# Sigmoid attention in 128-row chunks, with the last 64 rows of four heads as one float32 step in quarters of TensorE

## The chip, the cores and the metric

The kernel runs on one core of one Trainium2 chip. The metric is the device time of one execution in microseconds (us). Before the change three runs took 1105.21 to 1106.7 us, median 1105.92.

## The reference

Eight batches of twelve heads go through sigmoid attention, and the result through a two-layer perceptron with a gate. All inputs and outputs are float32 (the perceptron's weights reach the kernel as 64-bit floats and are decoded in it).

```
q, k, v: (8, 12, 448, 64)
scores = q @ k.T / sqrt(64) - log(448)
attn   = 1 / (1 + exp(-scores))
x      = (attn @ v), heads side by side: (3584, 768)
h      = x @ w_in                        # (768, 2048)
out    = (h / (1 + exp(-1.702 h))) @ w_out   # (2048, 768)
```

## The kernel before

Attention works on 48 pairs of heads, in the order of batches, six pairs in each. A pair's q and k lie side by side in one tile of 128 rows (two heads of 64 dimensions) by 896 columns, first the 448 of q, then the 448 of k. `split_pair` turns it into two float32r tiles, the rounded values (line 347) and the rest (line 358), both on VectorE; the first pair of all is used unrounded, in plain float32. A product of two split operands is then three float32r products: rest by rounded, rounded by rest, rounded by rounded.

k is cut into four chunks of 112 rows. For each chunk `scores` (line 541) multiplies the chunk, as weights of 64 rows by 112 columns, with q, for both heads: one head in the upper half of TensorE's rows, one in the lower, into two PSUM banks. That is six matmuls in a chunk. ScalarE applies the sigmoid to both heads at once (line 552), and `values` (line 564) multiplies the result with v in plain float32, one head in the left half of TensorE's columns and one in the right, with 112 rows. A profile shows each float32 matmul as two. The four chunks accumulate in one bank, whose two halves of rows are then the output of the two heads; ScalarE or VectorE copies it out into `x32` tiles (lines 598 and 600, `to_x`), which are stored to memory (`xd`).

A unit of work on TensorE is the four score chunks of one pair and behind them the four value chunks of the pair before. Scores and outputs take turns at four places of two PSUM banks each (`two_banks`).

Between the pairs the kernel decodes the perceptron's weights (lines 408 to 442, 32 pieces, each loaded by a transfer of 768 KB into one of three buffers `raw64`), forms sums of some of them (line 683) and stores the results. A load of weights is tied to the progress of the pairs by `PACE`. The order of all instructions on each engine and of the transfers on the SP queue is fixed when the kernel is built: `Plan.run` plays the tasks through with a cost for each and emits them in that order. So an instruction that waits holds back all that stand behind it on its engine. Tiles that come from a ring (`BUFS` has the sizes) wait for the last user of the tile that had the place.

Behind attention comes the perceptron, first for one block of 512 tokens (lines 716), then for pairs of blocks with fewer products (lines 952 and 1093). Its first products need six tiles `x0_0` to `x0_5`, loaded back from memory and split as well (lines 347 to 358).

## Time and profile before

| what | value |
|---|---|
| median of three runs | 1105.92 us |
| the profiled execution, its span | 1107.12 us, 1105.3 us |
| TensorE, VectorE, ScalarE busy in the span | 99%, 69%, 46% |
| granted TensorE clock | 1.00 |
| score matmuls (line 541) | 1128 in float32r, 127.3 us |
| value matmuls (line 564) | 768 records, 154.7 us |
| sigmoids of attention (line 552) | 192, 183.0 us |
| first perceptron product on TensorE | at 285.26 us |

Busy times of TensorE are those of overlapping matmuls. The page names engines PE (TensorE), PEld (its weight loads), DVE (VectorE), ACT (ScalarE) and SPq (the queue that issues transfers). A group of instructions reads: line, engine, operation, output<-inputs, shapes, count, busy time, mean ns of one, idle time of the engine just before and what ended it.

### The profile page before, as it was taken

The page shows a single profiled execution, that of the slowest core. Times are in us where ns is not written, and L with a number is a line of the kernel's source. Part 1 is how long each engine was busy: PE and PEld are TensorE (multiplying, and loading weights), DVE is VectorE, ACT ScalarE, POOL GpSimd, SP SyncE. Part 2 cuts the span into 40 slices and gives each one's busy share as a digit, 9 for nine tenths or more (in the row PEclk, how much of TensorE's full clock was granted, in tenths as well). Part 3 has the DMA queues.
Part 4 walks back from the last instruction along what each step waited for, and adds up shares of the span by engine and source line. Part 5 has one row for each costly group of instructions (what it writes and reads, how often), then busy time and mean ns, then how long its engine had stood idle before and what let it go on. Part 6 is the DMA issues. An engine that isn't in the chain of part 4 may idle for free.

```text
span 1105.3 us, 14979 instructions
## 1 busy us (share of the span) xinstructions
PE 1098.0 (99%) x5538; PEld 826.1 (75%) x5538; DVE 764.7 (69%) x1246; ACT 507.2 (46%) x717; POOL 0.2 (0%) x4
## 2 busy tenths in 40 slices
PE   9999999999999999999999999999999999999998
PEld 5455555555788888888888888888888888888887
DVE  6899999998597227887983764448955744487652
ACT  7888998888553222224532222225332222244220
POOL 0000000000000000000000000000000000000000
PEclk9999999999999999999999999999999999999999
DMA  9999999999647878676777876557679755556665
GB/s 311 324 367 358 359 390 382 374 340 336 196 161 247 312 243 296 243 257 212 233 226 249 300 236 199 194 193 240 219 228 305 254 188 190 187 182 207 201 212 187
DMA packets 113240, 285.68 MB, mean 258 GB/s; under 512 B 10384, under 2 KB 51472, under 8 KB 113168
## 3 DMA queue, kind: packets, MB, share of 16 engines
q1 hardware_dynamic: 113168, 284.73, 75.4%
q8 instruction: 44, 0.72, 0.3%
q14 instruction: 28, 0.23, 0.1%
HBM read 206.05 MB, written 78.64 MB: 258 GB/s over the span
## 4 chain that ended last, share of the span: by engine, by line
PE 95%; DMA 3%; DVE 1%; SPq 0%; issue 0%; DVEq 0%
PE os L1093 18%; PE m L952 18%; PE oa L1093 13%; PE av L564 12%; PE sc L541 10%; PE sc L952 9%; PE h L716 6%; PE o L716 6%; PE av L952 4%; DMA qkraw<-qk 2%; DMA w<-w 1%; SPq L326 0%; DVE qk L358 0%; DVE qk L347 0%; DVE expo L408 0%
## 5 line engine op out<-in xcount | busy, mean ns | idle before, releaser
L552 ACT ACTIVATE a<-sc,bias 112x896 f32<-112x896 f32 x192 | 183.0, 1005 | 33.7 <-PE av L564 19.9
L1093 PE MATMUL os<-gs,wds 128*128 128x512 f32 x864 | 196.3, 389 | 0.0
L1093 PEld LDWEIGHTS os<-gs,wds 128*128 128x128 f32 x864 | 162.2, 188 | 33.7
L564 PE MATMUL av<-a,vraw 112*64 112x448 f32 x768 | 154.7, 545 | 0.0
L1093 PE MATMUL oa<-ga,wda 128*128 128x512 f32 x648 | 147.4, 389 | 0.0
L1093 PEld LDWEIGHTS oa<-ga,wda 128*128 128x128 f32 x648 | 121.6, 188 | 25.3
L541 PEld LDWEIGHTS sc<-qk 64*112 64x112 f32 x1128 | 95.5, 171 | 48.9 <-ACT a L552 34.2
L541 PE MATMUL sc<-qk 64*112 64x448 f32 x1128 | 127.3, 370 | 2.4 <-DVE x L600 1.3
L564 PEld LDWEIGHTS av<-a,vraw 112*64 112x64 f32 x768 | 50.8, 136 | 82.7 <-issue 82.0
L952 PE MATMUL m<-x_s,w 128*128 128x512 f32 x468 | 109.3, 389 | 0.0
L952 PE MATMUL sc<-x,w 128*128 128x512 f32 x432 | 105.7, 389 | 0.0
L952 PEld LDWEIGHTS m<-x_s,w 128*128 128x128 f32 x468 | 87.8, 188 | 18.2
L952 PEld LDWEIGHTS sc<-x,w 128*128 128x128 f32 x432 | 81.1, 188 | 16.8
L914 ACT ACTIVATE g<-h 128x512 f32<-128x512 f32 x72 | 44.8, 633 | 90.6 <-DVE h L815 89.7
L352 ACT CAST gs<-gs 128x512 fp32r<-128x512 f32 x75 | 46.7, 623 | 84.3 <-PE os L1093 74.5
L716 PE MATMUL h<-x,wsplit 128*128 128x512 f32 x288 | 65.6, 389 | 0.0
L716 PE MATMUL o<-gs,wsplit 128*128 128x512 f32 x288 | 65.4, 389 | 0.0
L716 PEld LDWEIGHTS h<-x,wsplit 128*128 128x128 f32 x288 | 54.0, 188 | 11.9 <-issue 0.7
L716 PEld LDWEIGHTS o<-gs,wsplit 128*128 128x128 f32 x288 | 54.1, 188 | 11.2
L358 DVE TENSOR_TENSOR gs<-gs,gs 128x512 fp32r<-128x512 f32 x96 | 60.8, 685 | 0.4
L919 DVE TENSOR_TENSOR gs<-sc,g 128x512 f32<-128x512 f32 x24 | 16.6, 691 | 60.8 <-ACT g L914 60.8
L815 DVE TENSOR_TENSOR h<-h,m 128x512 f32<-128x512 f32 x36 | 24.7, 686 | 40.0 <-PE m L952 40.0
(93 smaller groups left out, 1237.2 us busy)
## 6 DMA issues: line engine op xcount, KB each, us to landing
w<-w SPq DMA_DIRECT2D x56, 768.0 KB, 6.7
wds<-t SPq DMA_DIRECT2D x72, 384.0 KB, 4.0
t<-t SPq DMA_DIRECT2D x32, 768.0 KB, 5.0
w<-t SPq DMA_DIRECT2D x32, 768.0 KB, 5.0
qkraw<-qk SPq DMA_DIRECT2D x47, 448.0 KB, 8.6
wda<-w SPq DMA_DIRECT2D x48, 384.0 KB, 3.9
f<-w SPq DMA_DIRECT2D x32, 384.0 KB, 5.9
w<-wsplit SPq DMA_DIRECT2D x16, 768.0 KB, 6.2
```

Source lines behind the costliest of these rows:

```text
L352: (costs[0], lambda: nc.scalar.copy(hi(), src())),
L358: lambda: nc.vector.tensor_tensor(lo(), src(), hi().bitcast(F32), op=ALU.subtract),
L541: nc.tensor.matmul(ps.tile[:C, j, :S], lhsT=src[kk][rows, S + c * C : S + (c + 1) * C], rhs=src[qq][rows, :S], start=n == 0, stop=n == len ...
L552: nc.scalar.activation(a.tile[:C, c % 2], ps.tile[:C, :, :S], AF.Sigmoid, bias=bias[:C], scale=scale)
L564: nc.tensor.matmul(ps.tile[cols, 0, :S], lhsT=vr.tile[:C, j, c], rhs=a.tile[:C, c % 2, j], start=c == 0, stop=c == NC - 1,)
L716: nc.tensor.matmul(ps, lhsT=ws[a], rhs=x[:, c], start=first and i == 0, stop=last and i == 2)
L815: nc.vector.tensor_tensor(out(), a(), b(), op=op)
L914: nc.scalar.activation(g.tile, h(), AF.Sigmoid, scale=1.702)
L919: nc.vector.tensor_tensor(gb.tile[:, block - one], h(), g.tile, op=ALU.mult)
L952: nc.tensor.matmul(ps, lhsT=ws[c], rhs=x[:, d], start=not more and i == 0 and j == 0, stop=i == NK // 2 - 1 and j == 2, skip_group_check=more,
L1093: nc.tensor.matmul(to, lhsT=w[c], rhs=x.tile[:, d], start=not more and i == 0 and j == 0, stop=i == len(rows) - 1 and j == 2, skip_group_c ...
```

## The change

Heads go by fours, as two pairs. k is cut into three chunks of 128 rows, and the 64 rows left over of each of the four heads form one further step (`scores_left`): four products with weights of 64 rows by 64 columns, each in one quarter of TensorE, in plain float32 from the raw q/k tiles, into two banks. One sigmoid serves all four. `values` works with 128 rows, and `values_left` adds the four heads' last 64 rows of v, again in quarters. The output of four heads shares one place of two banks (`bank` in `to_x`), and is copied out when `values_left` is done. v is laid out on the host so that one load brings four heads. The rounding of q and k may now go to ScalarE or VectorE. The PSUM places have new names (`q0` to `q3`), and the perceptron uses `q0` and `q1` where it used `sc`.

```diff
--- before.py
+++ after.py
@@ -34,15 +34,15 @@
 
 
 BUFS = dict(
-    qk=2, vraw=3, a=3, x32=8, x=6, g=16, line=4, wsplit=3, raw64=3, w32=2, e=4,
-    sc=2, sc3=1, sc4=1, av=1, m=2, m0=1,
+    qk=2, vraw=3, a=6, x32=8, x=6, g=16, line=4, wsplit=3, raw64=3, w32=2, e=4,
+    q0=1, q1=1, q2=1, q3=1, av=1, m=2, m0=1,
     xs=15, xa=4,
 )
 
 ATTENTION, LATE = ("qk", "vraw", "a", "raw64", "e"), ("xs", "xa")
 SHARED = ("line",)
 
-EARLY, SINGLE = ("sc3", "sc4"), ("m0", "av", "m")
+PAIRED, EARLY, SINGLE = ("q0", "q1"), ("q2", "q3"), ("m0", "av", "m")
 
 
 
...
@@ -257,8 +257,10 @@
     NW = w.shape[0]
     NF = NW * NK // (NK + NM)
 
-    NC = 4
-    C = S // NC
+    NC = S // P
+    C = S - NC * P
+
+    VC = (2 * NC + 1) * P
     NW_EL = NK * P
     scale = 1.0 / math.sqrt(D)
     neg_log_s = -math.log(S)
...
@@ -485,24 +488,29 @@
         n: [dram.tile([P, T], F32, name=f"xd{n}_{p}", tag=f"xd{n}_{p}") for p in range(NP)]
         for n in range(NB)
     }
-    spilled = {}
+    spilled, v_of = {}, {}
 
     def load_pair(b, p):
 
         tag = "x"
-        qkr, vr = buffer(tag), buffer("vraw")
-        vals, rows = v[b], C
+        qkr = buffer(tag)
+
         def first():
             if qkr.tile is None:
                 make(qkr, tag, [P, S2], F32, f"qkraw{b}_{p}")
 
 
         t_q = []
-        for cols in (slice(0, S + C), slice(S + C, S2)) if (b, p) == (0, 0) else (slice(0, S2),):
+        for cols in (slice(0, S + P), slice(S + P, S2)) if (b, p) == (0, 0) else (slice(0, S2),):
             t_q.append(dma(lambda cols=cols: qkr.tile[:, cols], lambda cols=cols: qk[b, p * P : (p + 1) * P, cols],
                            P * (cols.stop - cols.start) * 4 / 1024, [], [qkr], first))
-        t_v = dma(lambda: vr.tile[:rows], lambda: vals[:, 2 * p : 2 * p + 2], rows * 8 * D * 4 / 1024, [], [vr],
-                  lambda: make(vr, "vraw", [P, 2, NC, D], F32, f"vraw{b}_{p}"))
+
+        if p % 2 == 0:
+            vr = buffer("vraw")
+            t_v = dma(lambda: vr.tile, lambda: v[b, p // 2], P * VC * 4 / 1024, [], [vr],
+                      lambda: make(vr, "vraw", [P, VC], F32, f"vraw{b}_{p}"))
+            v_of[b, p // 2] = t_v, vr
+        t_v, vr = v_of[b, p // 2]
         return t_q, qkr, t_v, vr
 
     def split_pair(b, p, t_q, qkr):
...
@@ -510,63 +518,88 @@
             return t_q[0], qkr
         s = buffer("qk")
         t = round_and_rest(
-            (None, 0.63, 1.09), s, lambda: qkr.tile, t_q, [qkr],
+            (0.94, 0.63, 1.09), s, lambda: qkr.tile, t_q, [qkr],
             lambda: s.tile[:, 0], lambda: s.tile[:, 1],
             lambda: make(s, "qk", [P, 2, S2], F32R, f"qk{b}_{p}"),
         )
         return t, s
 
 
-    turns, last_early = itertools.count(), {}
-
-    def two_banks(b):
-        b.tag = ("sc", "sc", *EARLY)[next(turns) % 4]
-        plan.rings.setdefault(b.tag, []).append(b)
-        last_early[b.tag] = b
-
-    def scores(b, p, c, t_s, s, a):
-
-        ps = Buffer()
-        two_banks(ps)
-
-
-        plain = (b, p) == (0, 0)
-        terms = ((0, 0),) if plain else ((0, 1), (1, 0), (0, 0))
-
+    last_early = {}
+
+    def two_banks(place):
+        tag = (*PAIRED, *EARLY)[place % 4]
+        b = buffer(tag)
+        b.tag, last_early[tag] = tag, b
+        return b
+
+    def sigmoid(name, a, ps, t):
         def emit():
-            make(ps, ps.tag, [P, 2, 512], F32, f"sc{b}_{p}_{c}")
-            src = [s.tile] if plain else [s.tile[:, 0], s.tile[:, 1]]
-            for n, (kk, qq) in enumerate(terms):
+            make(a, "a", [P, 2, S], F32, name)
+            nc.scalar.activation(a.tile, ps.tile[:, :, :S], AF.Sigmoid, bias=bias, scale=scale)
+
+        return task("ACT", 1.02, emit, [t], [a, ps])
+
+    def scores(n, c, t_s, s, place):
+        ps, a = two_banks(place), buffer("a")
+
+        terms = ((0, 1), (1, 0), (0, 0)) if n else ((0, 0),)
+
+        def emit():
+            make(ps, ps.tag, [P, 2, 512], F32, f"sc{n}_{c}")
+            src = [s.tile[:, 0], s.tile[:, 1]] if n else [s.tile]
+            for i, (kk, qq) in enumerate(terms):
                 for j, rows in enumerate(halves_of_rows):
                     nc.tensor.matmul(
-                        ps.tile[:C, j, :S],
-                        lhsT=src[kk][rows, S + c * C : S + (c + 1) * C], rhs=src[qq][rows, :S],
-                        start=n == 0, stop=n == len(terms) - 1,
+                        ps.tile[:, j, :S], lhsT=src[kk][rows, S + c * P : S + (c + 1) * P], rhs=src[qq][rows, :S],
+                        start=i == 0, stop=i == len(terms) - 1,
                     )
 
-        t = task("PE", 0.9 if plain else (0.75, 0.61, 0.61, 0.61)[c], emit, t_s, [ps, s])
-
-        def sigmoid():
-            if a.tile is None:
-                make(a, "a", [P, 2, 2, S], F32, f"a{b}_{p}_{c}")
-            nc.scalar.activation(
-                a.tile[:C, c % 2], ps.tile[:C, :, :S], AF.Sigmoid, bias=bias[:C], scale=scale
-            )
-
-        return t, task("ACT", 1.02, sigmoid, [t], [a, ps])
-
-    def values(b, p, c, t_a, a, t_v, vr, ps):
+        t = task("PE", (0.7, 0.61, 0.61)[c] if n else 0.9, emit, t_s, [ps, s])
+        return t, sigmoid(f"a{n}_{c}", a, ps, t), a
+
+    def scores_left(n, sources, place):
+
+        ps, a = two_banks(place), buffer("a")
 
         def emit():
-            if c == 0:
-                make(ps, ps.tag, [P, 2, 512], F32, f"av{b}_{p}")
+            make(ps, ps.tag, [P, 2, 512], F32, f"sc{n}_{NC}")
+            for cols, (_, src) in zip(halves_of_rows, sources):
+                for j, rows in enumerate(halves_of_rows):
+                    nc.tensor.matmul(
+                        ps.tile[cols, j, :S], lhsT=src.tile[rows, S + NC * P :], rhs=src.tile[rows, :S],
+                        start=True, stop=True, skip_group_check=True,
+                    )
+
+        t = task("PE", 0.95, emit, [t for ts, _ in sources for t in ts], [ps, *(b for _, b in sources)])
+        return t, sigmoid(f"a{n}_{NC}", a, ps, t), a
+
+    def values(n, c, t_a, a, t_v, vr, ps):
+
+        def emit():
+            if ps.tile is None:
+                make(ps, ps.tag, [P, 2, 512], F32, f"av{n}")
             for j, cols in enumerate(halves_of_rows):
+                at = ((n % 2 * 2 + j) * NC + c) * D
                 nc.tensor.matmul(
-                    ps.tile[cols, 0, :S], lhsT=vr.tile[:C, j, c], rhs=a.tile[:C, c % 2, j],
-                    start=c == 0, stop=c == NC - 1,
+                    ps.tile[cols, n % 2, :S], lhsT=vr.tile[:, at : at + D], rhs=a.tile[:, j],
+                    start=c == 0, stop=False, skip_group_check=True,
                 )
 
-        return task("PE", (0.8, 0.75, 0.75, 0.85)[c], emit, [t_a, t_v], [ps, a, vr])
+        return task("PE", (0.8, 0.75, 0.75)[c], emit, [t_a, t_v], [ps, a, vr])
+
+    def values_left(t_a, a, t_v, vr, ps):
+
+        def emit():
+            for k, rows in enumerate(halves_of_rows):
+                for j, cols in enumerate(halves_of_rows):
+                    at = (4 * NC + j) * D
+                    nc.tensor.matmul(
+                        ps.tile[cols, k, :S], lhsT=vr.tile[rows, at : at + D], rhs=a.tile[rows, j],
+                        start=False, stop=True, skip_group_check=True,
+                    )
+
+        return task("PE", 0.95, emit, [t_a, t_v], [ps, a, vr])
 
     def places(b):
 
...
@@ -591,16 +624,20 @@
 
             yield block, xb, first, into, cols
 
+    copies = []
+
     def to_x(b, p, t, ps):
+        bank = (b * NP + p) % 2
         for block, xb, first, into, cols in x32_places(b, p):
             n = cols.stop - cols.start
-            wrote[block, p].append(on_either(
+            copies.append(on_either(
                 (0.2 + 0.00075 * n, lambda xb=xb, into=into, cols=cols: nc.scalar.copy(
-                    xb.tile[:, into], ps.tile[:, 0, cols])),
+                    xb.tile[:, into], ps.tile[:, bank, cols])),
                 (0.15 + 0.00105 * n, lambda xb=xb, into=into, cols=cols: nc.vector.tensor_copy(
-                    xb.tile[:, into], ps.tile[:, 0, cols])),
+                    xb.tile[:, into], ps.tile[:, bank, cols])),
                 [t], [xb, ps], first,
             ))
+            wrote[block, p].append(copies[-1])
         split_x(b, p)
 
     def split_x(b, p):
...
@@ -620,36 +657,50 @@
         ), x)
 
 
-    firsts = []
+    firsts, urgent = [], []
 
     def attention():
 
-        units, late = [], []
+
+
+
+
+
+        units, late, held = [], [], 0
         for n, (b, p) in enumerate(pairs):
             t_q, qkr, t_v, vr = load_pair(b, p)
             t_s, s = split_pair(b, p, t_q, qkr)
-            ps = Buffer()
-            scored, next_late = [], []
             firsts.append(t_s)
-            for half in range(2):
-                a = buffer("a")
-                got = [scores(b, p, c, [t_s] if n else t_q[: c + 1], s, a) for c in range(2 * half, 2 * half + 2)]
-                scored.append([g[0] for g in got])
-                next_late.append([
-                    values(b, p, 2 * half + i, g[1], a, t_v, vr, ps) for i, g in enumerate(got)
-                ])
-
-            if n:
-                two_banks(before)
-            before = ps
-
-            for t in scored[1] + [t for two in late for t in two]:
+            chunks = [scores(n, c, [t_s] if n else t_q[: c + 1], s, held + 1 + c) for c in range(NC)]
+            run = [t for t, _, _ in chunks]
+            if n % 2 == 0:
+                left, chunks0, pair0 = [(t_q, qkr)], chunks, (b, p)
+            else:
+                t_left, t_a, a = scores_left(n, [*left, (t_q, qkr)], held)
+                run.append(t_left)
+                held += 1
+                ps = two_banks(held)
+                both = [
+                    [values(m, c, got[1], got[2], t_v, vr, ps) for c, got in enumerate(cs)]
+                    for m, cs in ((n - 1, chunks0), (n, chunks))
+                ]
+                both[1].append(values_left(t_a, a, t_v, vr, ps))
+                late.append(both[0])
+                copied = len(copies)
+                for pair in (pair0, (b, p)):
+                    to_x(*pair, both[1][-1], ps)
+                urgent.append(copies[copied:])
+            if n > 2 and n % 2:
+
+                plan.early += [(t, run[0]) for t in urgent[n // 2 - 1]]
+
+            with_v = late.pop(0) if late else []
+            for t in run[2:] + with_v:
                 t.alone = False
-            units.append(scored[0] + scored[1] + [t for two in late for t in two])
-            to_x(b, p, next_late[1][1], ps)
-            late = next_late
-        two_banks(before)
-        units.append(late[0] + late[1])
+            units.append(run + with_v)
+            if n % 2:
+                late.append(both[1])
+        units.append(late.pop())
         return units
 
 
...
@@ -1183,7 +1234,12 @@
     DM, DF = moe_w_in.shape
     qk = np.concatenate([q, k], axis=2).transpose(0, 1, 3, 2)
     qk = np.ascontiguousarray(qk).reshape(B, H * D, 2 * S)
-    vl = v.reshape(B, H, 4, S // 4, D).transpose(0, 3, 1, 2, 4)
+
+
+    vh, full = v.reshape(B, H // 4, 4, S, D), S // P * P
+    chunks = vh[..., :full, :].reshape(B, H // 4, 4, full // P, P, D).transpose(0, 1, 4, 2, 3, 5)
+    ends = vh[..., full:, :].reshape(B, H // 4, 2, 2, S - full, D).transpose(0, 1, 2, 4, 3, 5)
+    vl = np.concatenate([chunks.reshape(B, H // 4, P, -1), ends.reshape(B, H // 4, P, 2 * D)], axis=3)
     vl = np.ascontiguousarray(vl)
     KB, FB = DM // P, DF // P
     wi = moe_w_in.reshape(KB, P, FB, P).transpose(2, 0, 1, 3)
```

In all, 47 roundings of q and k stood on VectorE before; now 30 do, and 17 on ScalarE. Of the copies out of PSUM 59 stood on VectorE and 25 on ScalarE; now 35 and 49. The two places that follow show the order itself.

TensorE in the middle of attention, before: `sc1_4_2` is the scores of batch 1, pair 4, chunk 2, `a` a sigmoid, `av` an output.

```order
L564 MATMUL av1_2_856<-a1_2_0_757,vraw1_2_686 64x448 x4
L564 MATMUL av1_2_856<-a1_2_2_804,vraw1_2_686 64x448 x4
L541 MATMUL sc1_4_0_878<-qk1_4_797 112x448 x6
L541 MATMUL sc1_4_1_892<-qk1_4_797 112x448 x6
L541 MATMUL sc1_4_2_900<-qk1_4_797 112x448 x6
L541 MATMUL sc1_4_3_910<-qk1_4_797 112x448 x6
L564 MATMUL av1_3_919<-a1_3_0_824,vraw1_3_753 64x448 x4
L564 MATMUL av1_3_919<-a1_3_2_867,vraw1_3_753 64x448 x4
```

The same place now: `sc13_0` is the scores of the pair numbered 13, chunk 0, and chunk 3 is the step of left-over rows; `av12` is the output of the pairs 12 and 13.

```order
L584 MATMUL av10_928<-a11_0_903,vraw1_4_650 64x448 x2
L584 MATMUL av10_928<-a11_1_916,vraw1_4_650 64x448 x2
L584 MATMUL av10_928<-a11_2_924,vraw1_4_650 64x448 x2
L597 MATMUL av10_928<-a11_3_939,vraw1_4_650 64x448 x4
L553 MATMUL sc13_0_1004<-qk2_1_926 128x448 x6
L553 MATMUL sc13_1_1017<-qk2_1_926 128x448 x6
L553 MATMUL sc13_2_1028<-qk2_1_926 128x448 x6
L569 MATMUL sc13_3_1038<-qkraw2_0_685 64x448 x2
L569 MATMUL sc13_3_1038<-qkraw2_1_687 64x448 x2
L584 MATMUL av12_1048<-a12_0_966,vraw2_0_763 64x448 x2
L584 MATMUL av12_1048<-a12_1_979,vraw2_0_763 64x448 x2
L584 MATMUL av12_1048<-a12_2_986,vraw2_0_763 64x448 x2
```

Each pair had four chunks of scores of 112 columns, then two times two chunks of values. Now it has three of 128, and in turn the left scores stand behind the chunks (`x2` for each pair's raw tile) or the left values behind the values (`x4`).

VectorE at the end of attention, before: `x32_6_2` is the copy out of a finished pair, `x0_3` the split of the perceptron's first input tiles, `w32_15` the last weights decoded.

```order
L424 TENSOR_TENSOR expo15_3205<-expo15_3205,sign15_3186 128x768
L358 TENSOR_TENSOR qk7_5_3250<-qkraw7_5_2872,qk7_5_3250 128x896
L600 COPY x32_6_2_2884<-av7_2_3247 128x448
L442 SCALAR_TENSOR_TENSOR w32_15_3200<-w32_15_3200,expo15_3205 128x768
L358 TENSOR_TENSOR x0_3_3144<-x0_3_3144 128x512
L353 CAST x0_4_3202<-x0_4_3202 128x512
L358 TENSOR_TENSOR x0_4_3202<-x0_4_3202 128x512
L358 TENSOR_TENSOR x0_5_3264<-x0_5_3264 128x512
L600 COPY x32_6_3_2947<-av7_3_3305 128x448
L600 COPY x32_6_4_3020<-av7_4_3353 128x448
```

The same place now; `av46` is the output of the last four heads.

```order
L411 TENSOR_SCALAR expo15_3121<-w64_15_2883 128x768
L443 SCALAR_TENSOR_TENSOR w32_15_3119<-w64_15_2883,w32_15_3119 128x768
L419 TENSOR_SCALAR expo15_3121<-expo15_3121 128x768
L636 COPY x32_6_5_2887<-av46_3095 128x448
L423 TENSOR_SCALAR expo15_3121<-expo15_3121 128x768
L427 TENSOR_TENSOR expo15_3121<-expo15_3121,sign15_3115 128x768
L361 TENSOR_TENSOR x0_2_2991<-x0_2_2991 128x512
L361 TENSOR_TENSOR x0_3_2994<-x0_3_2994 128x512
L445 SCALAR_TENSOR_TENSOR w32_15_3119<-w32_15_3119,expo15_3121 128x768
L361 TENSOR_TENSOR x0_4_3098<-x0_4_3098 128x512
L361 TENSOR_TENSOR x0_5_3101<-x0_5_3101 128x512
```

Tiles 3 to 5 of the perceptron's input were split ahead of the last copies. Now the copy out of the last four heads stands ahead of the splits of tiles 2 to 5.

More of the change, by code (lines that the diff above doesn't have):

```diff
@@ L277, in banks @@
         )
-    banks("sc", ctx)
+    for tag in PAIRED:
+        banks(tag, ctx)
     for tag in EARLY:
@@ L975, in copy @@
                 )
-            p1 = product(q, "sc", q0, w1, t_1, 0, "a11", [], False)
+            p1 = product(q, pair, q0, w1, t_1, 0, "a11", [], False)
             firsts_of[n] = [p1]
@@ L981, in up @@
             c4 = copy(h21, "h21", in_(w), p4, [w])
-            p2 = product(q, "sc", q0, w1, t_1, 1, "a12", [c1], True)
+            p2 = product(q, pair, q0, w1, t_1, 1, "a12", [c1], True)
             activated(one, f, q0, p2, [q])
@@ L1103, in products @@
                 return ends
-            three, other = ("sc", "sc", "av"), ("m0", "m", "m")
+            three, other = (*PAIRED, "av"), ("m0", "m", "m")
             def result(ps, bank):
-                return lambda: ps.tile[:, 0] if bank == "sc" else ps.tile
+                return lambda: ps.tile[:, 0] if bank in PAIRED else ps.tile
             def copies(tag, name, banks, bufs, ends):
```

18 lines of the change are left out of this document (9 added, 9 removed).

## The prediction

> **What bounds the kernel now.** I read the page's busy shares, then the chain of waits in order of time, then a table of stretches, then the timeline of one pair of heads. TensorE first: busy 99% of the span.
>
> ```profile
> PE 1098.0 (99%) x5538; PEld 826.1 (75%) x5538; DVE 764.7 (69%) x1246; ACT 507.2 (46%) x717; POOL 0.2 (0%) x4
> PE   9999999999999999999999999999999999999998
> DVE  6899999998597227887983764448955744487652
> ACT  7888998888553222224532222225332222244220
> DMA  9999999999647878676777876557679755556665
> ```
>
> The change touches attention, the first ten slices, where VectorE and the DMA engines are as full as TensorE and ScalarE is close. So the chain is asked which of them sets the pace (start, length, what).
>
> ```profile
> 5.37 10.50 DMA qkraw<-qk
> 18.02 12.61 DMA qkraw<-qk
> 30.70 10.78 DMA w<-w
> 47.72 3.16 PE av L564 x16
> ...
> 99.78 3.16 PE av L564 x16
> 102.93 2.63 PE sc L541 x24
> 105.57 3.16 PE av L564 x16
> ...
> 279.10 6.16 PE av L564 x32
> 285.26 65.51 PE h L716 x288
> ```
>
> Up to 47.7 us the chain runs through transfers and decoding; from there to the end it is TensorE alone: one pair of heads takes 3.16 + 2.63 = 5.79 us, four heads 11.58 us, without a break until the perceptron begins at 285.26 us. From 47.7 us there are 40 pairs, 20 fours. The neighbours are nearly as full (columns: busy of PE, PEld, DVE, ACT, POOL; clock; DMA share; GB/s):
>
> ```profile
> 83.00:110.00 27.00, 27.00 (x188) 14.23 (x186) 25.33 (x45) 23.91 (x28) 0.00 (x0) 1.00 0.98 357
> 166.00:193.00 27.00, 27.00 (x192) 14.69 (x190) 24.96 (x43) 22.99 (x29) 0.00 (x0) 1.00 1.03 381
> 249.00:276.00 27.00, 27.00 (x188) 14.10 (x184) 23.37 (x40) 21.73 (x27) 0.00 (x0) 1.00 0.95 340
> ```
>
> VectorE 25.3 of 27 (94%), ScalarE 89%, DMA 98 to 103%. TensorE leads by a few per cent only; this limits what it can gain.
>
> **The change part by part.** First TensorE. The unit prices come from these rows:
>
> ```profile
> 114.74 2.39 PE L541 MATMUL sc<-qk 64*112 64x448 f32 x22
> 145.69 0.37 PE L541 MATMUL sc<-qk 64*112 64x448 f32 x2
> 111.72 0.14 PEld L564 LDWEIGHTS av<-a,vraw 112*64 112x64 f32 x2 [0.23 <-issue]
> 112.09 0.14 PEld L564 LDWEIGHTS av<-a,vraw 112*64 112x64 f32 x2 [0.23 <-issue]
> 3.93 3.42 PE L541 MATMUL sc<-qkraw 64*112 64x448 f32 x16
> ```
>
> Rounded score products run two at a time, one in each half of the rows: 22 are 11 steps, and (2.39 - 0.37)/10 = 0.202 us a step. Float32 value products run two at a time in the halves of the columns, each recorded as two: weight loads come in pairs 0.375 us apart, so 0.75 us for a chunk of two heads. The plain float32 scores of the first pair (16 records, the first step slow) fit the same 0.375 in halves of the rows. A change of mode costs what remains: 3.16 - 8 x 0.375 = 0.16 us into values, 2.63 - 12 x 0.202 = 0.21 us into scores.
>
> Before, four heads are 2 x 12 score steps, 2 x 8 value steps and four changes: 11.6. After, they are 18 score steps, 12 value steps, two steps in quarters (left scores, left values) and six changes of mode. Twelve value steps: 4.50. Six changes at 0.16 to 0.21: 1.0.
>
> A quarter step isn't in this trace. It is four float32 products in two records each. From below, all four run at once: 2 x 0.375 = 0.75 us. From above, two at a time: 1.50 us. I take 0.75, which both float32 rows above are nearest to: halves of rows run at once, and so do halves of columns, each half with its own moving operand. The Trainium skill's page TensorEngine Tiling (Array Packing), section Tiling Modes, counts four independent tiles of 64x64, and by it the step is 0.75 too; the same section says that a change of mode drains TensorE, which speaks against the change: six drains for four. The measured 0.16 and 0.21 hold that drain, so that the sum has it.
>
> A score step loads 128 weight columns where it loaded 112. Two rows bound its price:
>
> ```profile
> L541 PEld LDWEIGHTS sc<-qk 64*112 64x112 f32 x1128 | 95.5, 171 | 48.9 <-ACT a L552 34.2
> L716 PEld LDWEIGHTS h<-x,wsplit 128*128 128x128 f32 x288 | 54.0, 188 | 11.9 <-issue 0.7
> ```
>
> The load of weights grows from 171 to about 188 ns, still under 202. From below the step stays 0.202. From above it is as long as the perceptron's steps with 128 columns: 65.51/288 = 0.227, which would follow if the load and a fixed gap after it set the step. I take 0.212, between, nearer to the row with the same 448 columns moving. 18 steps: 3.82 (3.64 to 4.09).
>
> Four heads after: 3.82 + 4.50 + 1.50 + 1.0 = 10.8 us against 11.58: 0.76 less (0.49 to 0.94). Over 20 fours: **-15.2 us** (-9.8 to -18.8). The first 47.7 us I give nothing, since transfers lead there (0 to -3).
>
> ScalarE and VectorE. Four heads have seven sigmoids, not eight, at 1.0 us. The order shows 17 of 47 roundings of q and k moved from VectorE to ScalarE, and 24 of the copies out of PSUM too.
>
> ```profile
> L552 ACT ACTIVATE a<-sc,bias 112x896 f32<-112x896 f32 x192 | 183.0, 1005 | 33.7 <-PE av L564 19.9
> L347 DVE CAST qk<-qkraw 128x896 fp32r<-128x896 f32 x47 | 29.2, 622 | 9.3 <-DMA qkraw<-qk 8.7 <-PE sc L541 0.5
> L600 DVE COPY x<-av x49: 219/480/625, 56.8 to 270.7; 128x320 f32<-128x320 f32 x12, 128x384 f32<-128x384 f32 x11, 128x128 f32<-128x128 f32 x6, 128x192 f32<-128x192 f32 x6
> ```
>
> VectorE loses 17 x 0.62 + 24 x 0.48 = 22 us over attention at most, less what comes back to it (15 of ScalarE's exponent steps, short ones); 94% of 5.79 is 5.44 us a pair, and 22/48 less is about 5.0 to 5.2, against TensorE's new 5.41. ScalarE loses 24 sigmoids of 1.0 and gains 17 casts of the same 896 columns, an estimated 1.0 at most, and 24 copies of 0.48 at most: 17 + 11.5 - 24 is +0.1 a pair on 89% of 5.79, so 5.2 at most. Both fit, at up to 96%. In order queues this full make each other late now and then; nothing shows how often. From below 0 (before, TensorE's steady stretch has no hole at 94%), from above 6 us (0.3 us in each four); I take **+2.5**. That also covers the left step, which waits for its two banks until the finished heads have been copied out: the three chunks ahead of it, 1.9 us, hide copies of some 2 x 0.48 = 1.0 on each of two engines; uncovered they cost a rival, below.
>
> Transfers: the bytes stay the same, v comes in 24 loads and not 48. A raw q/k tile is kept until the left step, so its ring of six runs less far ahead. That is affordable:
>
> ```profile
> 113.70 0.46 SPq L326 DMA_DIRECT2D qkraw<-qk  x1
> 146.43 0.62 DVE L347 CAST qk<-qkraw 128x896 fp32r<-128x896 f32 x1
> qkraw<-qk SPq DMA_DIRECT2D x32, 448.0 KB, 7.9
> ```
>
> The tile loaded at 113.70 us is first read 32.7 us later and lands after 7.9; two pairs less are some 21 us. Nothing added.
>
> The edge to the perceptron. Before, its first product follows the last value step with 0.7 us of weight-load idle. After, VectorE's order has the copy of the last heads, which must wait for the last value step, ahead of the rests of x tiles 2 to 5.
>
> ```profile
> L358 DVE TENSOR_TENSOR x<-x 128x512 fp32r<-128x512 f32 x24 | 15.7, 687 | 0.8 <-ACT x L352 0.7
> L424 DVE TENSOR_TENSOR expo<-expo,sign 128x768 bf16<-128x768 bf16 x32 | 17.6, 551 | 0.0
> L442 DVE SCALAR_TENSOR_TENSOR w<-w,expo 128x768 f32<-128x768 f32 x32 | 30.4, 952 | 0.0
> 100.56 0.35 DVE L416 TENSOR_SCALAR expo<-expo 128x768 uint16<-128x768 uint16 x1
> ```
>
> From the last value step: copy 0.62, 0.35, 0.55, two rests 1.37: tile 3 is ready at about 3.1 us with the signals; then 0.95 and two rests: tile 5 at 5.5. TensorE has 6 x 0.227 = 1.36 us of work in each pair of tiles: it waits about 1.6, then 1.0 us. Less the 0.7 of before: **+2** (0, if the copy is early, to +4, if the loads of tiles 4 and 5 are late as well). The later stages use the same banks under new names: nothing.
>
> Sum: -15.2 + 2.5 + 2 = -10.7, taken as -10. The profiled execution took 1107.1 us (its span 1105.3), 1.2 more than the median of the runs; -10 on the median of 1105.9 is **1096 us**.
>
> **The rivals.** *The DMA engines bind.* For it: shares of 0.95 to 1.03 from 55 to 276 us, and a decode whose load is used almost as it lands:
>
> ```profile
> 106.18 0.45 SPq L326 DMA_DIRECT2D w<-w  x1
> 115.90 0.55 DVE L435 TENSOR_SCALAR w<-w 128x768 uint32<-128x768 uint32 x1
> w<-w SPq DMA_DIRECT2D x23, 768.0 KB, 8.5
> GB/s 374 377 394 363 353 302 291 403 372 344 392 383 401 332 369 346 333 393 381 394 362 418 401 411 372 385 395 343 397 401 349 399 337 359 357 344 322 312 328 400
> ```
>
> 9.7 us from issue to use, 8.5 to land. Loads are tied to the pairs, so a pair that is 6% shorter asks for 6% more a second. If full engines can't give it, late weights hold VectorE in its order, and TensorE with it. Then only the unused share of the 221 us is gained (the three rows' mean is 0.987, so 3 us), and the edge takes 2 of it back: 1105 us, no change. Against it: the slices reach 418 where the mean is 367, raw q/k has 20 us to spare, so a queue may grow for a while, and the last sixth of attention is below full. The Trainium skill's page DMA: Bandwidth & Descriptors, section Specifications, puts a core's share of HBM at about 358 GB/s; taken as a ceiling, attention would not get shorter at all, but this trace moves 381 in one stretch, so it is no ceiling here.
>
> *Quarters run two by two*, the one on the slower side. Each of two quarter steps costs 1.50 us, four heads 12.3 against 11.58: +0.74 x 24 = 18 us, 1124 us. It turns from gain to loss where a quarter step exceeds 0.75 + 0.38 = 1.13 us. For it: no row shows four at once. Against it: both kinds of halves do run at once.
>
> *The left step waits for its banks.* Four heads leave PSUM together. If one engine does all four copies (4 x 0.48 = 1.9 us) behind an operation of 1.0, they end 1 us after the three chunks; at 0.5 us in each four that is another 10 us, 1104 us. From 0.4 on, little is left. Against it: the order spreads the copies over two engines and puts them ahead of the next roundings.
>
> **How the numbers follow.** My forecast 0.67; DMA binds 0.13; quarters two by two 0.11; banks 0.09. The likeliest alone has 1087 (-18.8, no friction) to 1104 (-9.8 + 6 + 2). The range 1084 to 1108 adds the 3 us of a shorter start below and the two mild rivals above, and leaves out the quarters. No change is within 0.2%, 2.2 us, about what a measurement of this kernel can tell. Faster: 0.65 of my own, 0.05 of the DMA case and 0.07 of the banks, 0.77. Slower: 0.11 of the quarters and 0.03 of the DMA case, where late weights cost more than they leave, 0.14. Same: the remaining 0.09.
>
> **What would show it.** In the chain after, 5.4 us a pair from about 45 us on; the left lines (L569, L597) with 8 records in about 0.75 us and their mode change, not 1.5; score steps at 0.20 (the load is hidden) or 0.227 (it sets the step); the perceptron's first product near 270 us, with two waits on VectorE of 1 to 2 us behind it. It is wrong if the waits of L438 or the signs on w loads grow to several us (DMA), if weight loads of L569 wait for the copies of L634 and L636 (banks), or if the quarter steps exceed 1.1 us.

## The result

Four runs of the changed kernel took 1088.29 to 1088.98 us, median 1088.53 us, beside four runs of the kernel before on the same chip with a median of 1106.31 us (1105.21 to 1107.24). The ratio is 0.984 (95% interval 0.9823 to 0.9857): 17.8 us, or 1.6%, faster. The forecast was 1096 us with a range of 1084 to 1108: the direction and the range held, and the gain was nearly twice the 10 us that were forecast.

The profiled execution of the changed kernel took 1088.40 us with a span of 1086.6 us, so its span is 18.7 us shorter than the 1105.3 us before. The explanation below accounts for these 18.7 us.

**The whole span.** The busy shares and slices of the page of after:

```profile
PE 1076.9 (99%) x5444; PEld 802.4 (74%) x5444; DVE 751.2 (69%) x1223; ACT 489.7 (45%) x716; POOL 0.2 (0%) x4
PE   8999999999999999999999999999999999999998
DVE  6999989987985248887865844458846644487652
DMA  9899999997649787667668775567779755556665
```

TensorE is still busy 99% of the span, with 21 us less busy time. VectorE and the DMA engines are as full in the first ten slices as before: the change took work off the leader and left the balance as it was.

**The steady stretch.** The timeline of TensorE in the middle of attention, after (start, length, what; L553 are the chunks of scores, L569 the left scores, L584 the values, L597 the left values):

```profile
131.35 2.09 PE L553 MATMUL sc<-qk 64*128 64x448 f32 x18
133.38 2.48 PE L584 MATMUL av<-a,vraw 128*64 128x448 f32 x12
135.78 0.98 PE L597 MATMUL av<-a,vraw 64*64 64x448 f32 x8
136.69 2.09 PE L553 MATMUL sc<-qk 64*128 64x448 f32 x18
138.72 0.98 PE L569 MATMUL sc<-qkraw 64*64 64x448 f32 x8
139.63 2.48 PE L584 MATMUL av<-a,vraw 128*64 128x448 f32 x12
142.03 2.09 PE L553 MATMUL sc<-qk 64*128 64x448 f32 x18
```

Lengths overlap, so the starts are subtracted. Four heads last from 131.35 to 142.03: 10.68 us, where before they took 11.58 by the sum and 11.56 by the starts. Each part can be read off: nine score steps with the change of mode in front of them 2.03 us, which is 9 x 0.202 + 0.21; six value steps 2.40, which is 6 x 0.375 + 0.15; a step in quarters 0.91, which is 0.75 + 0.16. (A change of mode is a change between tiles of half the rows, half the columns or a quarter of TensorE.) The eight records of a quarter step are two for each of the four products, and they fit into two times 0.375 us only if the four quarters run at once.

**The beginning and the end of attention.** The same view of before, then of after, at pair 9 (the first row of each), at pair 47, the last, and at the first product of the perceptron. Pairs are counted from 0 here, as in the name `sc13`; the recorded expectations count one less, so that their pair 8 is the row at 56.59 us.

```profile
56.59 2.70 PE L541 MATMUL sc<-qk 64*112 64x448 f32 x24
...
276.40 2.70 PE L541 MATMUL sc<-qk 64*112 64x448 f32 x24
...
285.19 2.12 PE L716 MATMUL h<-x,wsplit 128*128 128x512 f32 x8
```

```profile
51.25 2.09 PE L553 MATMUL sc<-qk 64*128 64x448 f32 x18
...
233.38 2.09 PE L553 MATMUL sc<-qk 64*128 64x448 f32 x18
236.66 0.98 PE L569 MATMUL sc<-qkraw 64*64 64x448 f32 x8 [1.20 <-ACT x L634]
...
256.00 2.09 PE L553 MATMUL sc<-qk 64*128 64x448 f32 x18
...
263.60 0.98 PE L597 MATMUL av<-a,vraw 64*64 64x448 f32 x8
264.51 1.65 PE L767 MATMUL h<-x,wsplit 128*128 128x512 f32 x6
267.35 1.65 PE L767 MATMUL h<-x,wsplit 128*128 128x512 f32 x6 [1.19 <-DVE x L361]
269.43 0.97 PE L767 MATMUL h<-x,wsplit 128*128 128x512 f32 x3 [0.43 <-DVE x L361]
```

| where | gained, us |
|---|---|
| up to pair 9: 56.59 to 51.25 | 5.34 |
| pairs 9 to 47, 19 fours at 0.88 to 0.90 | 16.9 |
| less two holes in that stretch, 0.56 and 1.27 (the larger is the row at 236.66) | -1.8 |
| pair 47 to the first product of the perceptron: 8.79 to 8.51 | 0.3 |
| less the two waits behind that product (267.35 and 269.43) | -1.95 |
| together | 18.7 |

The waits at the edge are those of the last two rows: there the distance from one product to the next is 1.59 and 0.81 us where it is 0.227 otherwise, together 1.95 us more. From there to the end both kernels take the same time. The chain of waits of after begins at the edge, with the split of an x tile on VectorE, and continues on TensorE:

```profile
269.43 62.86 PE h L767 x276
```

**The neighbours.** The table of stretches of after (busy of PE, PEld, DVE, ACT, POOL; clock; DMA share; GB/s), and from the page the weight loads of the score steps:

```profile
83.00:110.00 27.00, 27.00 (x196) 12.97 (x192) 24.40 (x43) 23.68 (x33) 0.00 (x0) 1.00 0.99 370
138.00:166.00 28.00, 28.00 (x202) 13.69 (x202) 26.12 (x44) 25.72 (x33) 0.00 (x0) 1.00 1.00 388
221.00:249.00 28.00, 26.80 (x196) 12.81 (x194) 22.99 (x40) 21.39 (x29) 0.00 (x0) 1.00 1.02 400
```

```profile
L553 PEld LDWEIGHTS sc<-qk 64*128 64x128 f32 x846 | 75.9, 184 | 39.7 <-ACT a L539 17.3
```

In these stretches VectorE is at 82 to 93%, ScalarE at 76 to 92%, and the full DMA engines moved 370 to 400 GB/s where the stretches shown of before had 340 to 381. The weight load of a score step grew from 171 to 184 ns, and the step stayed at 0.202 us.

### The profile page after: what moved, and what is told of

The parts are those of the page before. It is cut to its first block, busy times and chain, and to the rows that moved or that the text cites. A ratio compares the mean times of both kernels' runs of the same rounds, so it can differ in the third digit from the quotient of the medians.

```text
span 1086.6 us, 14787 instructions
## 1 busy us (share of the span) xinstructions
PE 1076.9 (99%) x5444; PEld 802.4 (74%) x5444; DVE 751.2 (69%) x1223; ACT 489.7 (45%) x716; POOL 0.2 (0%) x4
## 4 chain that ended last, share of the span: by engine, by line
PE 75%; DVE 0%; issue 0%
PE os L1144 18%; PE m L1003 18%; PE oa L1144 14%; PE q L1003 9%; PE o L767 6%; PE h L767 6%; PE av L1003 5%; DVE p L866 0%; DVE x L361 0%
## 5 line engine op out<-in xcount | busy, mean ns | idle before, releaser
L539 ACT ACTIVATE a<-sc,bias 128x896 f32<-128x896 f32 x168 | 159.7, 1017 | 14.2 <-PE sc L553 10.1
L584 PE MATMUL av<-a,vraw 128*64 128x448 f32 x576 | 118.6, 547 | 0.0
L1003 PE MATMUL q<-x,w 128*128 128x512 f32 x432 | 105.7, 389 | 0.0
L553 PEld LDWEIGHTS sc<-qk 64*128 64x128 f32 x846 | 75.9, 184 | 39.7 <-ACT a L539 17.3
L553 PE MATMUL sc<-qk 64*128 64x448 f32 x846 | 98.3, 373 | 1.8 <-DVE qk L361 1.8
L1003 PEld LDWEIGHTS q<-x,w 128*128 128x128 f32 x432 | 81.1, 188 | 16.8
L584 PEld LDWEIGHTS av<-a,vraw 128*64 128x64 f32 x576 | 37.1, 136 | 69.0 <-issue 53.0
L970 DVE TENSOR_TENSOR gs<-q,g 128x512 f32<-128x512 f32 x24 | 16.6, 691 | 61.0 <-ACT g L965 61.0
```

What stands on the lines that cost most here:

```text
L539: nc.scalar.activation(a.tile, ps.tile[:, :, :S], AF.Sigmoid, bias=bias, scale=scale)
L553: nc.tensor.matmul(ps.tile[:, j, :S], lhsT=src[kk][rows, S + c * P : S + (c + 1) * P], rhs=src[qq][rows, :S], start=i == 0, stop=i == len( ...
L584: nc.tensor.matmul(ps.tile[cols, n % 2, :S], lhsT=vr.tile[:, at : at + D], rhs=a.tile[:, j], start=c == 0, stop=False, skip_group_check=True,)
L970: nc.vector.tensor_tensor(gb.tile[:, block - one], h(), g.tile, op=ALU.mult)
L1003: nc.tensor.matmul(ps, lhsT=ws[c], rhs=x[:, d], start=not more and i == 0 and j == 0, stop=i == NK // 2 - 1 and j == 2, skip_group_check=more,
```

## Experiments

Two questions were left after this comparison. Where do the 5.3 us of the beginning come from, which the forecast had at nothing? And does TensorE alone set the pace, or do VectorE and ScalarE hold a part of it? Times are medians; each ratio is to the kernel before on the same chip. The changed kernel was not timed again beside them. The kernel before was, with medians of 1106.35 and 1106.51 us where it had 1106.31, so differences from the changed kernel are read only where they exceed 1 us. Each edit also makes the planner distribute the work anew. In the changed kernel ScalarE has 17 of the 47 roundings; it has 21 with v in 112 and 16 rows, 7 without the left values, 17 with the edge altered, and 25 in the two kernels with the left scores first.

**v in 128 rows in the kernel before.** The first suspicion for the beginning was the load of v, which had 112 rows before and 128 after.

```diff
-        vals, rows = v[b], C
+        vals, rows = v[b], P
...
+    vl = np.concatenate([vl, np.zeros((B, P - S // 4, H, 4, D), vl.dtype)], axis=1)
```

> The kernel before, with one thing changed: v is padded on the host to 128 rows, so that each load of v fills all 128 partitions (2 KB a row as before, 14% more bytes of v) and not 112. Nothing else moves. Theory: the 112-row loads slowed all transfers (in the stretch from 10 to 30 us the kernel before moved some 345 GB/s at a DMA share of 1.02 to 1.04, the changed one 412 at 1.02), and that held the first eight pairs back; then pair 8 begins 3 to 5 us earlier than at 56.6 us, the steady 11.56 us for two pairs stays, and the time falls to 1101 to 1103 us. Rival: the changed kernel's start was shorter because its pairs are; then nothing moves, 1105 to 1107 us.

It took 1105.27 us (1104.87 to 1106.14), ratio 0.9991 (0.9982 to 1.0): about 1 us less, at the edge of what the runs can tell. The stretches from 10 to 30 us and from 55 to 249 us, first of the kernel before, then of this one (the last column is GB/s):

```profile
10.00:30.00 20.00, 20.00 (x140) 10.64 (x138) 18.24 (x30) 17.82 (x21) 0.00 (x0) 1.00 1.03 344
55.00:249.00 194.00, 194.00 (x1346) 103.57 (x1344) 182.90 (x312) 173.11 (x209) 0.00 (x0) 1.00 1.01 367
```

```profile
10.00:30.00 20.00, 20.00 (x140) 10.38 (x138) 19.23 (x31) 18.03 (x22) 0.00 (x0) 1.00 1.03 410
55.00:249.00 194.00, 194.00 (x1348) 103.70 (x1346) 183.78 (x313) 175.94 (x212) 0.00 (x0) 1.00 0.99 370
```

In the first 30 us 19% more bytes a second go through at the same share of busy DMA engines; later the rates are nearly equal, though this kernel moves 14% more bytes for v. Pair 9 begins at 54.29 us, 2.3 earlier than before. What vanished are two holes of TensorE, which stand in the timeline of before and not in this kernel's (here with a row of VectorE between them):

```profile
39.83 0.86 PE L541 MATMUL sc<-qk 64*112 64x448 f32 x6 [0.35 <-DVE x L600]
...
41.49 0.56 DVE L435 TENSOR_SCALAR w<-w 128x768 uint32<-128x768 uint32 x1 [1.26 <-DMA w<-w]
...
46.85 0.86 PE L541 MATMUL sc<-qk 64*112 64x448 f32 x6 [0.99 <-DVE x L600]
```

There TensorE waited for a bank that VectorE had not yet copied out, because VectorE had waited for weights (1.26 us in the row between, 1.50 us at 34.47) and the copy stands behind them in its order. So the rows of v's load were worth 2.3 us of the start at most in the kernel before; the profiled span is 1103.1 us, 2.2 less, and the runs show about half of that.

**v in 112 and 16 rows in the changed kernel.** The reverse: the load of four heads is cut in two. (These lines are shortened: they don't show the sizes, the making of the tile, and that the value steps wait for both loads.)

```diff
-            t_v = dma(lambda: vr.tile, lambda: v[b, p // 2], ...)
+            t_v = [
+                dma(lambda rows=rows: vr.tile[rows], lambda rows=rows: v[b, p // 2, rows], ...)
+                for rows in (slice(0, 112), slice(112, P))
+            ]
```

> The changed kernel with each load of v in two transfers, of 112 rows and of 16 rows; the same bytes and the same rows of 3584 B. Theory (112-row transfers slow all others): the rate between 10 and 30 us falls from 412 towards 350 to 370 GB/s, the first eight pairs lose 2 to 5 us, and the steady part, where the DMA share is 1.00 to 1.01, may lose some more: 1090 to 1095 us. Rival (length of a row or the number of loads made the difference): 1088 to 1089.5 us.

It took 1088.05 us (1086.54 to 1091.63), ratio 0.9837 (0.9811 to 0.9863): no difference from the changed kernel that these runs can tell. Yet from 10 to 30 us the transfers did slow down (the changed kernel, then this one):

```profile
10.00:30.00 20.00, 20.00 (x143) 9.11 (x140) 17.78 (x29) 17.28 (x20) 0.00 (x0) 1.00 1.02 412
```

```profile
10.00:30.00 20.00, 20.00 (x145) 9.79 (x145) 15.88 (x26) 17.73 (x20) 0.00 (x0) 1.00 1.03 323
```

Pair 9 begins 1.7 us later than in the changed kernel (52.91 us, not 51.25) and pair 11 2.7 us later, but the two holes at pairs 37 and 43 are gone, so that pair 47 is only 0.9 us late, and the edge waits 0.4 us less. What the start loses the end gets back, with four more roundings on ScalarE. So the transfers were not what the change gained by as a whole.

**Without the left values.** This kernel leaves out the products of the sigmoids with the last 64 rows of v, in all heads; it does everything else.

```diff
-                    start=c == 0, stop=False, skip_group_check=True,
+                    start=c == 0, stop=c == NC - 1, skip_group_check=True,
...
-                both[1].append(values_left(t_a, a, t_v, vr, ps))
```

> The changed kernel without the step of left values: the last 64 rows of v are left out of the output. On TensorE that takes a quarter step and one change of mode out of each four heads, 0.91 us by the trace (from 146.46 to 147.375), 24 times. If TensorE alone sets attention's pace, 10.68 falls to 9.77 us for four heads and the time to 1088.5 - 22 = 1066.5 us. Rival (the next limit is close): VectorE is busy 94% of 10.68 = 10.0 us for four heads and the DMA engines are full; then four heads take 10.0 to 10.4 us and the time is 1073 to 1082 us, with TensorE waiting for VectorE or for w loads.

It took 1073.31 us (1072.3 to 1075.27), ratio 0.9703 (0.9688 to 0.9718), 15.2 us less than the changed kernel. In the steady stretch its period is 9.77 us, exactly 0.91 less, the length of the step that is gone: there TensorE alone sets the pace, and its neighbours keep up even with a pace that is 0.91 us faster and with 40 of the 47 roundings on VectorE. Over 24 fours that is 21.8 us, and the perceptron indeed begins at 241.56 us, 22.95 earlier. Then some 7 us are lost. Timeline of TensorE, and a stretch with the granted clock (the number behind the last bracket):

```profile
247.29 7.55 PE L766 MATMUL h<-x,wsplit 128*128 128x512 f32 x25 [2.71 <-DVE x L361]
255.25 2.11 PE L766 MATMUL h<-x,wsplit 128*128 128x512 f32 x8 [0.41 <-DVE wsplit L361]
...
283.08 7.11 PE L766 MATMUL h<-x,wsplit 128*128 128x512 f32 x30 [3.04 <-DVE g L802]
```

```profile
283.08:288.00 4.92, 4.92 (x22) 4.06 (x23) 4.34 (x8) 3.61 (x6) 0.00 (x0) 1.00 0.39 160
```

TensorE waits for VectorE, which has not finished its splits and the last weights; the chain of waits there leads through a transfer of 8.7 us as well, whose data VectorE wrote late. Behind the first hole 25 products take 7.55 us instead of some 6.0; behind the one of 3.04 us they keep their pace, and the clock is full. So attention can outrun VectorE, and the bill comes at the edge; how much of it is due to the ten more roundings on VectorE stays open.

**All roundings of q and k on VectorE.** The part of the change that moves 17 of 47 roundings to ScalarE is undone. (The planner also puts five more copies out of PSUM on VectorE, 40 and not 35.)

```diff
-            (0.94, 0.63, 1.09), s, lambda: qkr.tile, t_q, [qkr],
+            (None, 0.63, 1.09), s, lambda: qkr.tile, t_q, [qkr],
```

> The changed kernel with all roundings of q and k on VectorE again, as before the change. My account says that VectorE had the room: 17 x 0.62 = 10.5 us more over 24 fours is 0.44 us, 10.0 + 0.44 = 10.5 of 10.68 us. Theory: at 98% its order holds TensorE up now and then, 1 to 4 us, 1089.5 to 1092.5 us. Rival (TensorE's 10.68 is safe as long as VectorE stays below it): no change, 1088 to 1089 us. A large loss, over 6 us, would say that the moved roundings were the condition for the gain.

It took 1094.39 us (1093.87 to 1095.64), ratio 0.9893 (0.9878 to 0.9908): 5.9 us more than the changed kernel, a third of the gain. The steady period is 10.68 us as before. The loss lies in few places (timeline of TensorE):

```profile
237.45 0.98 PE L569 MATMUL sc<-qkraw 64*64 64x448 f32 x8 [2.49 <-ACT sign L415]
238.37 4.17 PE L584 MATMUL av<-a,vraw 128*64 128x448 f32 x12
...
271.50 2.08 PE L767 MATMUL h<-x,wsplit 128*128 128x512 f32 x6 [2.86 <-DVE x L361]
274.25 6.99 PE L767 MATMUL h<-x,wsplit 128*128 128x512 f32 x19 [0.66 <-DVE x L361]
```

A hole of 2.49 us (1.20 in the changed kernel), and at the edge 2.86 and 0.66 (1.19 and 0.43). But the products behind the holes are longer as well: twelve value records take 4.17 us instead of 2.48, and 19 products take 6.99 where 19 x 0.227 + 0.3 = 4.6 would be usual. The table of stretches tells why:

```profile
238.40:241.80 3.40, 3.40 (x13) 1.19 (x12) 3.30 (x7) 1.01 (x1) 0.00 (x0) 0.51 1.02 411
271.50:274.20 2.70, 2.08 (x6) 1.17 (x6) 2.70 (x6) 0.00 (x0) 0.00 (x0) 0.70 0.43 163
274.20:278.80 4.60, 4.55 (x11) 3.63 (x12) 2.19 (x3) 1.33 (x2) 0.00 (x0) 0.50 0.62 203
```

By narrower stretches TensorE had half its clock from 238.4 to 241.9 us and from 272.6 to 279.4 us. The two slow stretches cost 1.7 and about 2.8 us, 4.5 of the 7.3 us by which this profiled span is longer. In the other three runs the mean granted clock was 0.996 to 0.998, not 0.995, so they lost less to it. Moving the roundings is therefore worth more than the room on VectorE: in the changed kernel it keeps the holes short.

**The roundings alone, in the kernel before.** The opposite edit, at the same place of the kernel before: (None, 0.63, 1.09) becomes (0.94, 0.63, 1.09).

> The kernel before, with one part of the change alone: the rounding of q and k may go to ScalarE or VectorE. Nothing is left out. Theory (before, TensorE alone sets the pace from 47.7 us on, and the engines beside have enough room): the period of four heads stays 11.56 us, the time within 2 us of 1106.3, at most a start that is 1 us shorter. Rival (the relief of VectorE is worth something by itself, as the changed kernel without it is 5.9 us longer): 1101 to 1104 us.

It took 1119.14 us (1118.71 to 1119.33), ratio 1.0111 (1.0096 to 1.0126): 12.6 us slower than the kernel before, which neither theory had. Attention does what the theory said: its period stays 11.56 us, and its start is 1.7 us shorter. The loss comes behind it (TensorE's waits from 285 to 335 us, the group of the last step of the decode on VectorE in that stretch, and an earlier stretch):

```profile
PE h L716 <- DVE g L752: 11.7, 2, 11.4
```

```profile
L442 DVE SCALAR_TENSOR_TENSOR w<-w,expo 128x768 f32<-128x768 f32 x9 | 8.4, 952 | 0.0
```

```profile
249.00:276.00 27.00, 27.00 (x188) 14.19 (x184) 14.98 (x22) 21.46 (x25) 0.00 (x0) 1.00 0.49 140
```

Eleven of the 32 pieces of weights are decoded after the perceptron has begun at 283.50 us, nine of them in this stretch; in the kernel before none is. The kernel fixes VectorE's order, and in it a gate (g) that TensorE needs stands behind the decode. VectorE had the time earlier: it was busy 15.0 of the 27 us from 249 to 276, and the DMA engines half. So the room was there and the order did not use it. Behind the hole 36 products take 9.97 us instead of some 8.3, at half the clock in part. What in the planner's costs put the decode so late wasn't tried.

**The edge.** The loads of the six x tiles which the perceptron needs first are planned as landing 4 us earlier. That changes the order, and it moves one copy: in VectorE's timeline the rests of tiles 2 and 3 are now done at 262.6 us and those of 4 and 5 at 266.8, where they were done at 267.9 and 270.0, and the copy of the last heads, which stood ahead of them on VectorE, is now on ScalarE, like the other one.

```diff
+EDGE = 4.0
...
+        t.landing -= EDGE if block == 0 else 0.0
```

> The changed kernel, with one number of the planner altered: the loads of the six x tiles that the perceptron needs first are planned as landing 4 us earlier, so that VectorE's order has the rests of tiles 2 to 5 ahead of the copy of the last heads, as before the change. Nothing is left out. Theory (the two waits of 1.6 and 0.8 us behind the first perceptron product are the price of that order): they vanish, 2 us less, 1086.5 us. Rival (VectorE has a backlog at the end of attention, the order only moves it): the waits turn up elsewhere between 255 and 285 us, perhaps as a later last copy or last sigmoid, and the time stays within 1 us of 1088.5.

It took 1086.18 us (1085.69 to 1086.72), ratio 0.9814 (0.9799 to 0.9828), 2.35 us less than the changed kernel. The waits are gone, and the products run on from the first:

```profile
263.35 0.98 PE L599 MATMUL av<-a,vraw 64*64 64x448 f32 x8
264.26 8.00 PE L770 MATMUL h<-x,wsplit 128*128 128x512 f32 x34
```

So the two waits were the price of that order, and VectorE's backlog, which is one copy smaller here, did not put them elsewhere.

**The left scores behind the left values.** In the odd pairs the left scores move ahead of the chunks, next to the other step in quarters, so that a change of mode is saved. (These lines don't show that the sigmoids of the left step get a buffer of their own, one of the six of `a`.)

```diff
-            chunks = [scores(n, c, [t_s] if n else t_q[: c + 1], s, held + 1 + c) for c in range(NC)]
+            odd = n % 2
+            if odd:
+                t_left, t_a, a = scores_left(n, [*left, (t_q, qkr)], held + 1)
+            chunks = [scores(n, c, [t_s] if n else t_q[: c + 1], s, held + 1 + odd + c) for c in range(NC)]
...
-                t_left, t_a, a = scores_left(n, [*left, (t_q, qkr)], held)
-                run.append(t_left)
+                run.insert(0, t_left)
```

> The changed kernel, with the left-over scores of the odd pair moved ahead of its three chunks, directly behind the left-over values of the four heads before, both in quarters of TensorE: five changes of mode in four heads and not six. The sigmoids of the left step get a buffer of their own. Nothing is left out. Theory (TensorE alone sets the steady pace, and a change of mode costs 0.16 to 0.21 us): the period of four heads goes from 10.68 to about 10.5 us, and over some 22 fours the perceptron begins 3.5 to 4 us earlier; of that the edge, where VectorE is behind, takes some back: 1085 to 1087 us. Rival (two steps of quarters in a row still pay a change between different sizes of operands, or the rounding rate of the engines beside sets the pace): the period stays 10.68 and the time 1088.5.

It took 1084.13 us (1083.67 to 1085.48), ratio 0.9798 (0.9782 to 0.9814), 4.4 us less than the changed kernel. Timeline of TensorE:

```profile
133.64 0.98 PE L597 MATMUL av<-a,vraw 64*64 64x448 f32 x8
134.44 0.93 PE L569 MATMUL sc<-qkraw 64*64 64x448 f32 x8
135.30 2.09 PE L553 MATMUL sc<-qk 64*128 64x448 f32 x18
```

The two quarter steps together take 1.66 us where they took 2 x 0.91 = 1.82. The period is 10.51 instead of 10.68: a change of mode is worth 0.16 to 0.17 us, as the forecast had it. Over 22 fours that is 3.7 us; the holes at pairs 37 and 43 are gone too, 1.8 us, and the perceptron begins at 258.47 us, 6.0 earlier. The edge takes 1.6 of it back, since its waits now are 0.74 and 2.42 us.

**Both together.** The edits of the last two kernels, nothing else.

> Both alterations together: the left-over scores directly behind the left-over values, and the first six x tiles planned as landing 4 us earlier. Nothing is left out. Theory (a shorter period, and an edge without waits, add up): 1082.5 to 1085 us. Rival (VectorE's backlog at the end of attention takes the gain, as it took a third of what leaving out the left-over values gave): 1086 to 1088 us, with holes of TensorE between 250 and 285 us.

It took 1080.31 us (1080.04 to 1080.61), ratio 0.9761 (0.9746 to 0.9775): 8.2 us less than the changed kernel and 26 us less than before, the fastest of all. This is better than either theory gave. The end of attention has no hole:

```profile
257.71 0.98 PE L599 MATMUL av<-a,vraw 64*64 64x448 f32 x8
258.62 3.72 PE L772 MATMUL h<-x,wsplit 128*128 128x512 f32 x15
```

The perceptron begins 5.9 us earlier than in the changed kernel, and the 1.95 us of waits are gone: 7.8 us, as the spans say (1086.6 and 1078.8). The edit of the edge is worth 2.35 us alone and 3.8 us here, as there is more to wait for.

## Why the prediction was right, and where it was off

**What bounds the kernel: right.** TensorE sets the pace of the steady stretch, in both kernels. Taking 0.91 us out of its work in four heads shortened four heads by 0.91, and taking a change of mode out by 0.17.

**Score steps: the right mechanism, the size at the lower bound.** 0.212 us was taken, between 0.202 (the load of weights is hidden) and 0.227 (it sets the step). The load grew to 184 ns and stayed hidden: 0.202. With 18 steps in four heads that is 0.18 us less than taken; the period came out as 10.68, not the 10.8 of the sum, and the steady stretch gave 16.9 us in 19 fours, not 15.2 in 20.

**Steps in quarters: right.** 0.75 us and a change of mode of 0.16, by the starts. The rival in which they run two by two fell. The Trainium skill's page TensorEngine Tiling (Array Packing), section Tiling Modes, has four independent tiles of 64x64 and a drain when the mode changes; this trace agrees with the first, and with the second in that a change costs time: 0.16 to 0.17 us is what one change less was worth.

**"The first 47.7 us I give nothing": the step that failed.** The beginning gave 5.34 us, where the forecast had 0 to 3. The chain of waits of before ran through transfers up to 47.7 us, and from that I concluded that less work on TensorE could not help there. The starts of the pairs say something else: from pair 2 to pair 9 the kernel before had two holes of TensorE, and the rest was TensorE at its steady pace. Of the 5.34 us, 0.83 is gained up to pair 3 (20.04 and 19.21 us), three fours from there to pair 9 give 0.88 each, 2.65, and the two holes are 1.87. The holes were VectorE's copies, late behind the transfers; the kernel before loses them with faster loads of v as well as with roundings on ScalarE. A chain that runs through a transfer shows what the last wait hung on, and not that the whole stretch is the transfer's.

**Friction: +2.5 taken, 1.8 measured.** Two holes, 0.56 and 1.27 us, both at the left step, which is the rival of the banks in small. At the second one (the row at 236.66) ScalarE's last copies out of the bank stand behind two sigmoids:

```profile
234.48 1.91 ACT L539 ACTIVATE a<-sc,bias 128x896 f32<-128x896 f32 x2
236.27 0.34 ACT L634 COPY x<-av 128x64 f32<-128x64 f32 x2
```

At the first, before the left step at 203.36 us, VectorE's last copies end at 203.26, behind a rest of 1.08 us. Both holes are absent in two of the variants, with v in two loads and with the left scores first; these have four and eight more roundings on ScalarE, so whether it is the order or the room on VectorE isn't shown. The estimate that both neighbours fit at up to 96% held.

**The edge: +2 taken, 1.95 measured, in part by luck.** The waits on the named rests came, and the experiment on the edge shows that the order made them. But each wait ended with the first rest of its pair of tiles, 2 and 4 (done some 0.6 us before 3 and 5), so they were 1.95 us together where the sum had 1.6 + 1.0. And the 0.7 us taken off were idle time of the weight load alone: before the change TensorE's first product follows the last value step without a hole, so there was nothing to take off. The two errors cancel.

**Moved work of the neighbours: counted as harmless, in fact a condition.** The forecast asked only whether ScalarE and VectorE fit. The roundings on ScalarE are worth 5.9 us in the changed kernel, a good part of it by the clock behind longer holes. The steady stretch doesn't need them; the last third of attention does, where VectorE has the decode and the first splits as well. In the kernel before the same permission costs 12.6 us. Its worth hangs on the order that the planner makes of it.

**DMA: the rival fell, by its own sign.** The shares stayed at 0.99 to 1.02, and the rate rose to 370 to 400 GB/s. A share of one was no ceiling, since the duration of a packet is not fixed: from 10 to 30 us the engines were full at 323 GB/s with v in 112 and 16 rows and at 412 in the changed kernel.

**Sum.** Forecast -10 (its terms gave -10.7), measured -18.7 in the span. The difference of 8.0 is 5.3 from the beginning, 2.0 from the steady stretch and the last pairs (17.2 against 15.2) and 0.7 from the friction.

## What to carry to other kernels

Ask of each stretch what its engine does between its holes: a chain that names a transfer doesn't exclude that shorter work makes the stretch shorter. When the leader of a balanced kernel gets less work, look for the bill where an in-order neighbour has its backlog, here the edge to the next stage; it may be only an order to be mended, and the mended order with one change of mode less gave another 8 us. Steps of the same tile shape belong next to each other.

## What the hardware showed that was not expected

- **The clock can fall after a short hole, and its length alone doesn't decide.** Behind holes of TensorE of 2.49 and 2.71 us the granted clock was half for 3.4 us, and behind one of 2.86 us, followed by a second of 0.66, for 6.8 us; products took 0.43 us instead of 0.227. It fell 0.1 to 1.1 us after the hole had ended. In the hole of 11.4 us (the roundings alone, in the kernel before) it fell inside and was half for 10.2 us, so that the slow stretches are one, two and three times 3.4 us long. Behind holes of 1.20, 2.42 and 3.04 us it stayed at 1.00. So the hole of 2.49 us cost about 4.2, and the one of 3.04 us no more than itself. The Trainium skill's page TensorE: Matmul & The Clock Gate, section What's actually happening, has the halved clock and an idle window of about 3.4 us that runs freely; the half and the 3.4 us agree, and here idle times shorter than that window were enough, but not each time.
- **The shape of one load can slow all.** From 10 to 30 us, with 112 rows in the load of v (of 128 possible), the core's transfers ran at 344 GB/s in the kernel before and at 323 in the changed one (there as 112 and 16 rows); with 128 rows at 410 and 412, at the same busy share of the DMA engines. From 55 to 249 us it doesn't show: 367 and 370 GB/s in the two kernels of before. Why isn't shown. The Trainium skill's page DMA: Bandwidth & Descriptors, section Specifications, puts a core's share of HBM at about 358 GB/s; here one core alone moved over 400.
